# A gated GELU feed-forward kernel: the opening loads dealt out as two equal lines, and five w_down blocks in two transfers each

## The chip, the cores and the metric

The kernel runs on one core of a Trainium2 chip. The metric is the device time of one execution in microseconds (us); lower is better. The kernel before takes 591.58 us, the median of three runs that lie between 591.08 and 591.84 us. One further execution was taken with the hardware profiler on; all durations below come from that one.

## The reference

The inputs are bfloat16: x of 2048 tokens by 1024, w_gate and w_up of 1024 by 3584, w_down of 3584 by 1024.

```python
def _gelu(x):
    return jax.nn.gelu(x, approximate=True)

def reference(x, w_gate, w_up, w_down):
    g = jnp.einsum("bsd,df->bsf", x, w_gate)
    u = jnp.einsum("bsd,df->bsf", x, w_up)
    h = _gelu(g) * u
    return jnp.einsum("bsf,fd->bsd", h, w_down)
```

Three matrix products, with a gated GELU between the first two and the third. The GELU is the tanh form, which the kernel computes as the gate value times a sigmoid of a cubic in it.

## The kernel before, in words

The tokens are worked in two halves of 1024, each in two chunks of 512. For a half, the kernel first computes the hidden values h (kept transposed in `hT`, hidden features on the partitions) and then the output rows of that half.

**Hidden values.** The 3584 hidden features are 28 blocks of 128, in eight groups of 3, 3, 3, 3, 4, 4, 4, 4 blocks (`GROUPS`). For one block and one chunk, eight matmuls of 128x512 (one for each 128 of the 1024 model dimensions, index `ko`, function `mm1`, L103) add up the gate value in one PSUM bank, and eight more the up value in another. ScalarE (ACT) and VectorE (DVE) then form GELU(gate) x up in five operations (class `Evac`) and write it to `hT`. The weights of a group stand in one of three ring buffers (`wg`, `wu`) and are loaded ahead by SyncE's DMA queue (SP), one transfer of gate and one of up weights for a group (`wload`, L89).

**Output.** For each 128 tokens and each 512 output columns, 28 matmuls with `hT` as the stationary side and `wd` (w_down, seven blocks of four 128-row slices each) as the moving side fill one bank (`down`, L306); the bank is copied and stored (`store`). The seven `wd` blocks are loaded once, one 1 MB transfer each, between the weight prefetches of the first half (L326).

**The order of the work.** The schedule is by hand: each engine's and each queue's instructions run in the order in which the program names them. DMAs are issued from two queues, SP and ACT's own (ACT's DMA issues stand in ACT's program order between its other instructions). A DMA signals its landing on one of eight DMA semaphores, which are handed out in turn; a DMA that takes over a semaphore waits until that semaphore's last DMA has landed.

**The opening,** which the change is about. The moving side of the first products is x transposed (`xT`). For the first chunk, six of the eight 128-wide slices of x are loaded plainly, in three pieces `xn` of 512 tokens by 256 (`xpart`, L186), and turned on TensorE: the function `turn(ko)` makes four 128x128 transposes against an identity matrix (L230) into a PSUM bank, and DVE copies them into `xT` (L236; for `ko` = 0 in two copies of 256 columns each, L239 and L240). The last two slices come by transposing DMA (`xload`, L98). The weights of group 0 come in single slices of 128x384 for `ko` 0 to 3 and in double slices after that (`wpart`, L192). The fifteen opening loads are dealt to the two queues in a hand-written order (L200 to L214): SP has the first x piece (all 512 tokens), then an up slice, the second x piece, and so on; ACT has the first two gate slices, an up slice, the third x piece, and so on.

Before the data is there, TensorE runs six filler matmuls on constants (`dummy`, L174; `NWARM`). ACT loads its activation table (L180) and does one 1-element Square on the tile `gate` (L181), which DVE has zeroed (L178, 128x512 bfloat16); ACT's later DMA issues stand behind these two in its program. In `first_group`, TensorE runs `turn(0)`, two more fillers of 512 and 256 columns while DVE copies, the three gate matmuls of `ko` = 0, `turn(1)`, the three up matmuls of `ko` = 0, and then for each further `ko` two matmuls, the next `turn`, and four matmuls. The loop that sets this order:

```python
            for i, (b, j) in enumerate(steps):
                mm1(ps[j][b], (wg, wu)[b], j, 0, ko)
                if i == (2 if ko == 0 else 1) and ko + 1 < NTURN:
                    turn(ko + 1)
```

Of the kernel before, what the change touches and what calls it, by code (L numbers as in the profile page):

```python
# [14 lines left out]
def kernel(  # L15
# [36 lines left out]
    NTMP = 3  # L52
    NST = 4
    WDF = 4
    NWARM = 6
    NTURN = 6
    TPC = SCH // P

    pool = ctx.enter_context(tc.tile_pool(name="sb", bufs=1))
# [39 lines left out]
            out=xT[c][ko], in_=x2[s0 : s0 + SCH, ko * P : (ko + 1) * P]  # L99
        )  # L100

    def mm1(ps, w, j, c, ko):
        nc.tensor.matmul(  # L103
            ps,
            lhsT=w[:, ko, j * P : (j + 1) * P],
            rhs=xT[c][ko],
            start=(ko == 0),
            stop=(ko == NKB - 1),
        )

# [56 lines left out]

    ctx.enter_context(tc.manual_schedule())

    gate = pool.tile([P, SCH], bf16, name="gate")  # L170
    gated = pool.tile([P, 1], f32, name="gated")

    def dummy(b, n=SCH):
        nc.tensor.matmul(b[:, :n], lhsT=warm[:, :P], rhs=warm[:, :n], start=True, stop=True)  # L174

    nc.vector.memset(gate, 0.0)  # L178
    make_identity(nc, ident)
    nc.scalar.preload_act_table(ACT.Sigmoid)  # L180
    nc.scalar.activation(gated, gate[:, :1], ACT.Square)  # L181
    for _ in range(NWARM):
        dummy(banks[5])

    def xpart(eng, ko, n):
        eng.dma_start(  # L186
            out=xn[ko // 2][:, :, (ko % 2) * P : (ko % 2 + n) * P],
            in_=x2[0:SCH, ko * P : (ko + n) * P].rearrange("(t p) d -> p t d", p=P),
        )

    def wpart(eng, ring, w, ko, n):
        eng.dma_start(  # L192
            out=ring[0][:, ko : ko + n, : GROUPS[0] * P],
            in_=w[ko * P : (ko + n) * P, : GROUPS[0] * P].rearrange("(ko ki) f -> ki ko f", ki=P),
        )


    S, A = nc.sync, nc.scalar
    G, U = (wg_ring, w_gate), (wu_ring, w_up)
    xpart(S, 0, 2)  # L200
    wpart(A, *G, 0, 1)
    wpart(S, *U, 0, 1)
    wpart(A, *G, 1, 1)
    wpart(A, *U, 1, 1)
    xpart(S, 2, 2)
    xpart(A, 4, 2)
    wpart(S, *G, 2, 1)
    wpart(S, *U, 2, 1)
    wpart(S, *G, 3, 1)
    wpart(A, *U, 3, 1)  # L210
    wpart(S, *G, 4, 2)
    wpart(A, *U, 4, 2)
    wpart(S, *G, 6, 2)
    wpart(A, *U, 6, 2)  # L214
    for ko in range(NTURN, NKB):
        xload(0, 0, ko)
    for n in (1, 2):
# [32 lines left out]
    def first_group():  # L250
        wg, wu = wg_ring[0], wu_ring[0]
        ps = [(bank(), bank()) for _ in range(GROUPS[0])]
        turn(0)
        dummy(banks[5])
        dummy(banks[5], SCH // 2)
        n0 = GROUPS[0]
        for ko in range(NKB):
            steps = [(b, j) for j in range(n0) for b in range(2)]
            if ko == 0:
                steps = [(b, j) for b in range(2) for j in range(n0)]  # L260
            for i, (b, j) in enumerate(steps):
                mm1(ps[j][b], (wg, wu)[b], j, 0, ko)
                if i == (2 if ko == 0 else 1) and ko + 1 < NTURN:
                    turn(ko + 1)
        e = [Evac(ps[j][0], ps[j][1], j, 0) for j in range(GROUPS[0])]
        e[0].square()
        e[1].square()
        e[0].cubic()
        e[0].sigmoid()
        e[1].cubic()  # L270
        e[2].square()
        e[0].gelu()
        e[0].product()
        e[1].sigmoid()
        e[2].cubic()
        e[1].gelu()
        e[1].product()
        e[2].sigmoid()
        e[2].gelu()
        e[2].product()  # L280
# [34 lines left out]
    for half in range(NHALF):  # L315
        base = half * NG
        if half == 0:
            first_group()
            group(1, [0], ahead=2)
            group(2, [0])  # L320
            for g in range(NG):
                group(g, [1] if g < NW else range(HSC))
                i = g - 1
                if 0 <= i < len(wd):
                    for q in range(i, len(wd) if g == NG - 1 else i + 1):
                        nc.sync.dma_start(  # L326
                            out=wd[q],
                            in_=w_down[q * WDF * P : (q + 1) * WDF * P, :].rearrange(
                                "(fo fi) d -> fi fo d", fi=P
                            ),  # L330
                        )
                prefetch(g + 3)
        else:
            for g in range(NG):
                group(base + g, range(HSC))
                prefetch(base + g + 3)
        k = 0
        xnext = [(c, ko) for c in range(HSC) for ko in range(NKB)] if half + 1 < NHALF else []
        for ss in range(HS // P):
            for dc in range(NDC):  # L340
                last = half == NHALF - 1 and ss == HS // P - 1 and dc == NDC - 1
                if last:
                    down(half, ss, dc * DMW, DMW // 2, 1)
                    down(half, ss, dc * DMW + DMW // 2, P, 1)
                    down(half, ss, dc * DMW + DMW - P, P, 0)
                else:
                    down(half, ss, dc * DMW, DMW, k)
                k += 1
                if xnext:
                    c, ko = xnext.pop(0)  # L350
                    xload(half + 1, c, ko)
# [30 lines left out]
```

## Time and profile before

| what | value |
|---|---|
| median of three runs | 591.58 us (591.08 to 591.84) |
| the profiled execution's own time | 591.7 us |
| its span, first to last instruction | 589.9 us |
| TensorE (PE) busy | 583.4 us, 99% |
| DVE busy / ACT busy | 244.2 us (41%) / 147.7 us (25%) |
| matmuls of the gate and up products (L103), mean | 380 and 379 ns |
| matmuls of the output (L306), mean | 366 ns |
| fillers (L174), mean | 601 ns |
| first matmul with real data / last instruction on PE | 4.86 us / about 587.3 us |

How to read it: a duration of one matmul overlaps that of the next, so the pace of a row of matmuls is the distance between their starts (for 128x512, about 0.216 us in nearly all of the span), not the mean duration. "PEld" is TensorE's loading of the stationary side, which runs beside the matmuls. "SPq" and "ACTq" are the DMA issues of the two queues; their durations are those of the issue, not of the transfer.

### The profile page before, as it was taken

How to read it: one execution, taken by the hardware profiler on the slowest of the kernel's cores; microseconds unless marked ns; L12 is line 12 of the kernel's file. 1: busy time of each engine (PE TensorE's matmuls, PEld its weight loads, DVE VectorE, ACT ScalarE, POOL GpSimd, SP SyncE). 2: the span in 40 equal slices, each digit the busy share in tenths (PEclk: the TensorE clock that was granted, in tenths of full speed). 3: DMA queues.
4: the chain of work that ended last, by engine and by line, in shares of the span. 5: the costliest groups of instructions: out<-in, count | busy, mean ns of one | idle time of the engine just before them, and what ended most of it. 6: DMA issues, size and time to landing. Idle time of an engine off the chain costs nothing.

```text
span 589.9 us, 6587 instructions
## 1 busy us (share of the span) xinstructions
PE 583.4 (99%) x2723; PEld 269.0 (46%) x2776; DVE 244.2 (41%) x361; ACT 147.7 (25%) x243; POOL 0.7 (0%) x6
## 2 busy tenths in 40 slices
PE   9999999999999999999999999999999999999998
PEld 4444444444444444444444444444444444444445
DVE  1765665565656400000046565656556562000000
ACT  1433333333333200000023333333333331000000
POOL 0000000000000000000000000000000000000000
PEclk9999999999999999999999999999999999999999
DMA  8906936055050311111203034214000000000000
GB/s 233 222 10 186 316 104 214 13 202 178 1 178 1 107 48 42 45 46 36 54 19 108 17 126 143 86 57 131 12 1 1 1 2 9 19 27 19 27 19 27
DMA packets 57789, 45.51 MB, mean 77 GB/s; under 512 B 15776, under 2 KB 54176, under 8 KB 57760
## 3 DMA queue, kind: packets, MB, share of 16 engines
q1 hardware_dynamic: 56112, 44.05, 24.8%
q10 hardware_dynamic: 1648, 1.05, 0.6%
q8 instruction: 21, 0.34, 0.2%
q14 instruction: 8, 0.07, 0.0%
HBM read 37.49 MB, written 4.19 MB: 71 GB/s over the span
## 4 chain that ended last, share of the span: by engine, by line
PE 98%; DMA 1%; issue 0%; ACT 0%
PE bank L103 65%; PE bank L306 33%; DMA xn<-in_x_dram 1%; PE bank L230 0%; PE bank L174 0%; ACT st L298 0%
## 5 line engine op out<-in xcount | busy, mean ns | idle before, releaser
L103 PE MATMUL bank<-xT,wg 128*128 128x512 bf16 x880 | 213.8, 380 | 0.9
L103 PE MATMUL bank<-xT,wu 128*128 128x512 bf16 x876 | 212.6, 379 | 1.0
L306 PE MATMUL bank<-wd,hT 128*128 128x512 bf16 (+2 forms) x935 | 193.0, 366 | 0.9
L306 PEld LDWEIGHTS <-hT 128*128 128x128 bf16 x952 | 90.9, 98 | 102.9
L103 PEld LDWEIGHTS <-wg 128*128 128x128 bf16 x896 | 87.8, 98 | 105.6 <-issue 0.6
L103 PEld LDWEIGHTS <-wu 128*128 128x128 bf16 x896 | 87.7, 98 | 105.0
L125 ACT ACTIVATE sq<-bank 128x512 f32<-128x512 f32 x112 | 66.7, 596 | 172.7 <-PE bank L103 166.8
L136 DVE TENSOR_TENSOR tt<-sg,bank 128x512 bf16<-128x512 bf16 x112 | 77.0, 687 | 75.9 <-ACT sg L133 75.8
L128 DVE SCALAR_TENSOR_TENSOR wq<-sq,bank 128x512 f32<-128x512 f32 x112 | 76.9, 687 | 65.2 <-ACT sq L125 65.2
L133 ACT ACTIVATE sg<-wq 128x512 bf16<-128x512 f32 x112 | 70.5, 629 | 88.3 <-DVE wq L128 88.3
L300 DVE CAST st<-bank 128x512 bf16<-128x512 f32 (+2 forms) x17 | 11.1, 652 | 178.3 <-PE bank L306 166.9
L139 DVE TENSOR_TENSOR hT<-tt,bank 128x512 bf16<-128x512 bf16 x112 | 77.0, 687 | 12.4 <-DVE tt L136 0.9
L298 ACT CAST st<-bank 128x512 bf16<-128x512 f32 (+1 forms) x17 | 9.6, 566 | 178.1 <-PE bank L306 178.1
L236 DVE COPY xT<-bank 128x512 bf16<-128x512 bf16 x5 | 2.1, 425 | 6.2 <-PE bank L230 6.2
L174 PE MATMUL bank<-const-bfloat16-1.0 128*128 128x512 bf16 (+1 forms) x8 | 3.6, 601 | 0.8 <-PEq L366 0.8
L230 PEld LDWEIGHTS <-xn 128*128 128x128 bf16 x24 | 2.1, 111 | 2.7 <-DMA xn<-in_x_dram 1.2
L230 PE MATMUL bank<-ident,xn 128*128 128x128 bf16 x24 | 2.7, 247 | 0.3 <-DMA xn<-in_x_dram 0.3
L174 PEld LDWEIGHTS <-const-bfloat16-1.0 128*128 128x128 bf16 x8 | 1.0, 138 | 1.8 <-issue 1.8
L239 DVE COPY xT<-bank 128x256 bf16<-128x256 bf16 x1 | 0.3, 292 | 3.1 <-PE bank L230 3.1
L180 ACT ACT_TABLE_LOAD x1 | 1.3, 1283 | 0.7 <-PEq L366 0.7
L178 DVE MEMSET gate<- 128x256 uint32 x1 | 0.3, 272 | 0.9 <-PEq L366 0.9
masks.py:199 POOL TENSOR_SCALAR_AFFINE_SELECT ident<-ident 128x128 bf16<-128x128 bf16 x1 | 0.3, 292 | 0.1
(7 smaller groups left out, 1.1 us busy)
## 6 DMA issues: line engine op xcount, KB each, us to landing
wg<-in_w_gate_dram SPq DMA_DIRECT2D x8, 1024.0 KB, 5.4
wu<-in_w_up_dram SPq DMA_DIRECT2D x8, 1024.0 KB, 7.0
wd<-in_w_down_dram SPq DMA_DIRECT2D x7, 1024.0 KB, 8.8
wg<-in_w_gate_dram SPq DMA_DIRECT2D x7, 768.0 KB, 4.7
wu<-in_w_up_dram SPq DMA_DIRECT2D x7, 768.0 KB, 6.6
out_dram<-st SPq DMA_DIRECT2D x31, 128.0 KB, 1.7
xn<-in_x_dram SPq DMA_DIRECT2D x2, 256.0 KB, 4.0
xT<-in_x_dram SPq DMA_TRANSPOSE x26, 2.6
```

The costliest lines, as they stand in the source:

```text
L103: nc.tensor.matmul(ps, lhsT=w[:, ko, j * P : (j + 1) * P], rhs=xT[c][ko], start=(ko == 0), stop=(ko == NKB - 1),)
L125: nc.scalar.activation(self.sq, self.g, ACT.Square, scale=GELU_SQRT_C)
L128: nc.vector.scalar_tensor_tensor(out=self.wq, in0=self.sq, scalar=1.0, in1=self.g, op0=ALU.add, op1=ALU.mult)
L133: nc.scalar.activation(self.sg, self.wq, ACT.Sigmoid, scale=GELU_K)
L136: nc.vector.tensor_tensor(out=self.tt, in0=self.sg, in1=self.g, op=ALU.mult)
L139: nc.vector.tensor_tensor(out=self.dst, in0=self.tt, in1=self.u, op=ALU.mult)
L174: nc.tensor.matmul(b[:, :n], lhsT=warm[:, :P], rhs=warm[:, :n], start=True, stop=True)
L230: nc.tensor.transpose(tp[t // (TPC // 2)][:, t * P : (t + 1) * P], xn[ko // 2][:, t, (ko % 2) * P : (ko % 2 + 1) * P], ident,)
L236: nc.vector.tensor_copy(out=xT[0][ko], in_=tp[0][:, :SCH])
L298: nc.scalar.copy(out=st[:, :cw], in_=ps[:, :cw])
L300: nc.vector.tensor_copy(out=st[:, :cw], in_=ps[:, :cw])
L306: nc.tensor.matmul(ps[:, :cw], lhsT=hT[f][:, ss * P : (ss + 1) * P], rhs=wd[f // WDF][:, f % WDF, c0 : c0 + cw], start=(f == 0), stop=(f = ...
```

## The change

- **Opening loads.** Each of the three x pieces is issued as two transfers: the first 256 tokens by SP, the last 256 tokens by ACT (`xhalves`). All gate slices of group 0 go by SP, all up slices by ACT. Both queues thus have the same list: x half, slice 0, slice 1, x half, slice 2, slice 3, x half, slices 4-5, slices 6-7. There are 18 opening loads in place of 15.
- **ACT's start.** The table load and the 1-element Square come after ACT's first x half and ahead of its other loads. The `gate` tile that the Square waits for is twice as long (128x1024).
- **TensorE's opening.** `NWARM` goes from 6 to 7, but the loop runs `NWARM - 1` times, so there are six fillers as before. The two fillers after `turn(0)` are of 256 and 128 columns in place of 512 and 256. The three gate matmuls of `ko` = 0 become six of 256 columns: first the first 256 tokens for the three blocks, then the last 256 tokens. `turn(1)` still follows the gate matmuls.
- **w_down.** Five of the seven `wd` blocks are loaded as two transfers of two slices each (`NSPLIT = 5`); the other two stay whole.

In the compiled changed kernel, the semaphore waits of the opening loads are these. On SP, the first five loads wait for nothing, the sixth (gate slice 3) waits for one half of the first x piece, the third x half for gate slice 0, gate slices 4-5 for SP's half of the second x piece, gate slices 6-7 for gate slice 2. On ACT, the first three wait for no DMA (the second and third stand behind the Square), the half of the second x piece waits for a half of the first, up slice 2 for gate slice 1, up slice 3 for up slice 0, the half of the third x piece for up slice 1, up slices 4-5 for the half of the second x piece, up slices 6-7 for up slice 2. From the stores of the first half on, each transfer has the same semaphore as before, since the added transfers are eight in all.

```diff
-    NWARM = 6
+    NWARM = 7
     NTURN = 6
+    NSPLIT = 5
...
-    def mm1(ps, w, j, c, ko):
+    def mm1(ps, w, j, c, ko, t0=0, t1=SCH):
         nc.tensor.matmul(
-            ps,
+            ps[:, t0:t1],
             lhsT=w[:, ko, j * P : (j + 1) * P],
-            rhs=xT[c][ko],
-            start=(ko == 0),
+            rhs=xT[c][ko][:, t0:t1],
+            start=(ko == 0 and t0 == 0),
             stop=(ko == NKB - 1),
         )
...
-    gate = pool.tile([P, SCH], bf16, name="gate")
+    gate = pool.tile([P, 2 * SCH], bf16, name="gate")
...
-    nc.scalar.preload_act_table(ACT.Sigmoid)
-    nc.scalar.activation(gated, gate[:, :1], ACT.Square)
-    for _ in range(NWARM):
+    for _ in range(NWARM - 1):
         dummy(banks[5])
-    def xpart(eng, ko, n):
+    def xpart(eng, ko, n, t0=0, t1=TPC):
         eng.dma_start(
-            out=xn[ko // 2][:, :, (ko % 2) * P : (ko % 2 + n) * P],
-            in_=x2[0:SCH, ko * P : (ko + n) * P].rearrange("(t p) d -> p t d", p=P),
+            out=xn[ko // 2][:, t0:t1, (ko % 2) * P : (ko % 2 + n) * P],
+            in_=x2[t0 * P : t1 * P, ko * P : (ko + n) * P].rearrange("(t p) d -> p t d", p=P),
         )
...
+    def xhalves(ko, n):
+        xpart(S, ko, n, 0, TPC // 2)
+        xpart(A, ko, n, TPC // 2, TPC)
+
     G, U = (wg_ring, w_gate), (wu_ring, w_up)
-    xpart(S, 0, 2)
-    wpart(A, *G, 0, 1)
-    wpart(S, *U, 0, 1)
-    wpart(A, *G, 1, 1)
-    wpart(A, *U, 1, 1)
-    xpart(S, 2, 2)
-    xpart(A, 4, 2)
-    wpart(S, *G, 2, 1)
-    wpart(S, *U, 2, 1)
-    wpart(S, *G, 3, 1)
-    wpart(A, *U, 3, 1)
-    wpart(S, *G, 4, 2)
-    wpart(A, *U, 4, 2)
-    wpart(S, *G, 6, 2)
-    wpart(A, *U, 6, 2)
+    xhalves(0, 2)
+    nc.scalar.preload_act_table(ACT.Sigmoid)
+    nc.scalar.activation(gated, gate[:, :1], ACT.Square)
+    for ko in (0, 1):
+        wpart(S, *G, ko, 1)
+        wpart(A, *U, ko, 1)
+    xhalves(2, 2)
+    for ko in (2, 3):
+        wpart(S, *G, ko, 1)
+        wpart(A, *U, ko, 1)
+    xhalves(4, 2)
+    for ko in (4, 6):
+        wpart(S, *G, ko, 2)
+        wpart(A, *U, ko, 2)
...
-        dummy(banks[5])
         dummy(banks[5], SCH // 2)
+        dummy(banks[5], P)
...
-            steps = [(b, j) for j in range(n0) for b in range(2)]
+            steps = [(b, j, 0, SCH) for j in range(n0) for b in range(2)]
             if ko == 0:
-                steps = [(b, j) for b in range(2) for j in range(n0)]
-            for i, (b, j) in enumerate(steps):
-                mm1(ps[j][b], (wg, wu)[b], j, 0, ko)
-                if i == (2 if ko == 0 else 1) and ko + 1 < NTURN:
+                h = SCH // 2
+                steps = [(0, j, t, t + h) for t in (0, h) for j in range(n0)]
+                steps += [(1, j, 0, SCH) for j in range(n0)]
+            for i, (b, j, t0, t1) in enumerate(steps):
+                mm1(ps[j][b], (wg, wu)[b], j, 0, ko, t0, t1)
+                if i == (2 * n0 - 1 if ko == 0 else 1) and ko + 1 < NTURN:
                     turn(ko + 1)
...
-                        nc.sync.dma_start(
-                            out=wd[q],
-                            in_=w_down[q * WDF * P : (q + 1) * WDF * P, :].rearrange(
-                                "(fo fi) d -> fi fo d", fi=P
-                            ),
-                        )
+                        n = WDF // 2 if q < NSPLIT else WDF
+                        for f in range(0, WDF, n):
+                            r = (q * WDF + f) * P
+                            nc.sync.dma_start(
+                                out=wd[q][:, f : f + n, :],
+                                in_=w_down[r : r + n * P, :].rearrange("(fo fi) d -> fi fo d", fi=P),
+                            )
```

## The prediction, made before the changed kernel was run

> **What bounds the kernel now.** I read the page's busy shares first, then the chain of work that ended last.
>
> ```profile
> PE 583.4 (99%) x2723; PEld 269.0 (46%) x2776; DVE 244.2 (41%) x361; ACT 147.7 (25%) x243; POOL 0.7 (0%) x6
> ...
> PE bank L103 65%; PE bank L306 33%; DMA xn<-in_x_dram 1%; PE bank L230 0%; PE bank L174 0%; ACT st L298 0%
> ```
>
> TensorE carries the span. The one other thing on the chain is the load of an x piece. The chain in order of time says where:
>
> ```profile
> 0.67 0.07 issue
> 0.74 3.03 DMA xn<-in_x_dram
> 3.81 0.61 PE bank L230 x4
> 4.42 0.64 PE bank L174 x2
> 5.06 1.28 PE bank L103 x3
> 6.34 0.38 PE bank L230 x4
> ```
>
> After 3.81 us nothing but TensorE stands on it until the last store. So only the opening can be shortened, and a late transfer can only cost there if TensorE comes to stand still. The timeline of the opening (start, duration, engine, line, operation):
>
> ```profile
> 0.74 0.45 SPq L186 DMA_DIRECT2D xn<-in_x_dram  x1
> ...
> 0.77 2.72 PE L174 MATMUL bank<-const-bfloat16-1.0 128*128 128x512 bf16 x6 [0.77 <-PEq L366]
> ...
> 3.79 0.39 ACTq L186 DMA_DIRECT2D xn<-in_x_dram  x1
> ...
> 3.81 0.61 PE L230 MATMUL bank<-ident,xn 128*128 128x128 bf16 x4 [0.32 <-DMA xn<-in_x_dram]
> ...
> 4.22 0.84 PE L174 MATMUL bank<-const-bfloat16-1.0 128*128 128x512 bf16 x2
> ...
> 4.25 0.29 DVE L239 COPY xT<-bank 128x256 bf16<-128x256 bf16 x1 [3.12 <-PE bank L230]
> ...
> 4.86 1.48 PE L103 MATMUL bank<-xT,wg 128*128 128x512 bf16 x3
> ...
> 6.14 0.58 PE L230 MATMUL bank<-ident,xn 128*128 128x128 bf16 x4
> ...
> 6.56 0.81 PE L103 MATMUL bank<-xT,wu 128*128 128x512 bf16 x3
> ...
> 7.67 0.39 PE L230 MATMUL bank<-ident,xn 128*128 128x128 bf16 x4
> ```
>
> To be seen: x lands at 3.77 (0.74 + 3.03), TensorE's turn starts at 3.81. The first copy ends at 4.25 + 0.29 = 4.54, but the first real matmul comes only at 4.86, as the two fillers end there (4.22 + 0.43 + 0.21). Up to 6.14 matmuls run at half pace: three take (6.14 - 4.86) / 3 = 0.427 us each, against (6.99 - 6.56) / 2 = 0.215 later. The switch falls near 6.5. So a start moved forward by d within this slow stretch puts d of work at half pace ahead of the switch and saves only d / 2.
>
> The queues' view of the first 40 us, one value per us, and the time from issue to landing of the three x loads:
>
> ```profile
> GB/s 0 17 190 340 229 335 327 291 285 331 249 55 192 328 346 353 332 328 325 327 334 308 83 65 261 113 99 131 119 59 85 0 0 0 0 0 0 0 0 0
> ...
> DMA to landing us min/median/max: 3.0/4.2/5.0
> ```
>
> From 3 to 11 us the engines move about 300 GB/s; before 3 us they are not full.
>
> **The change part by part.** All against the profiled execution: 591.7 us, its span of 589.9 and 1.8 around it; it stands 0.12 over the median.
>
> *Fillers and the first matmuls.* The fillers shrink from 0.64 to 0.32 us, so they end at 4.22 + 0.32 = 4.54, and the first half matmul needs only the first copy, also done at 4.54. The hand-over from DVE to TensorE is hidden here; I take 0.06 us, from the distance of the end of the last 0.11 us transpose of the first half to the copy's start, bounds 0 and 0.2. The start comes at 4.60, 0.26 earlier: worth 0.13 at half pace (0.03 to 0.16). Six matmuls of 256 columns take 6 x 0.213, as three of 512 take 3 x 0.427: nothing. They load weights three more times; a weight load is 0.15 us here and the transposes, at 0.107 us each with a load of their own, hide theirs, so nothing (upper bound 3 x 0.15 uncovered, half of it 0.22).
>
> *The first x piece on two queues.* Both halves are issued at 0.74 (ACT's program now begins with its half). By 3 us 17 + 190 = 207 KB had moved, of the 262 KB of the piece, and the third microsecond ran at 190 against 340 in the fourth. If the second line fills that room, the piece comes up to 0.4 us sooner; TensorE could use 0.5, as its six fillers end at 0.77 + 0.38 + 5 x 0.427 = 3.29. If the start was slow for a reason that two lines share, it lands at 3.77 as now. Against it, SP's gate slice 0 (98 KB, 0.3 us at 330 GB/s) is now right behind SP's half and competes with ACT's half: up to 0.3 later. So -0.4 to +0.3 on landing; I take 0.2 earlier, between a full gain and none, since the slow stretch is visible: worth 0.10 (0.20 to -0.15).
>
> The rule that speaks against it: the Trainium skill, page "DMA: Bandwidth & Descriptors", section "Rules for kernel authors", says of two transfers to disjoint halves not to bother, since both run over the same sixteen engines and only interleave, and that spreading over issuing engines saves issue time alone. By that rule the 0.10 is gone and the sum is 591.45; the row with 190 GB/s leaves both open.
>
> *The weights of ko = 0 and 1.* Gate slice 0 landed by 4.1 before the first matmul at 4.86. Now SP sends it behind 131 KB rather than beside 262 KB; the bytes ahead of its end are no more than before, so about 4.1, against 4.40 needed. Up slice 0 is needed only at about 6.1.
>
> *ACT's start.* Its table load (1.28 us) moves behind an issue of 0.45; ACT has no other work until the first Square at 16.31. The doubled memset (0.27 to 0.54 us, starting at 0.86) ends at 1.40 instead of 1.13 and with the Square behind it holds ACT's next issue, as 1.17 follows 1.13 now. Up slice 0 thus goes out at 1.44. Nothing: 4.6 us lie between that and its use.
>
> *The second x piece.* SP's half goes out at about 2.3, like the whole piece now (1.79). ACT's half waits for a first half to land, at about 3.6, as ACT's x load now waits until 3.79. From issue to landing the x loads take 3.0 to 5.0; the issues of 98 KB on ACT 2.9 to 4.4. With 131 KB on a short queue I take 3.1, near the low end (the first gate slice 2.9, the first x piece 3.0): landed at 6.7. TensorE wants it at 7.67 less about 0.25, 7.4. Margin 0.7; at 5.0 it is late by 1.2 and that counts in full, since by then the pace is full. Behind it on ACT queue up slices 2 and 3, the third x half and the double slices; if all are 1 us later, up slices 4-5 (9.05 landed before, used at 12.01) still have cover. Nothing, bounds 0 and +1.2.
>
> *SP and its followers.* SP has nine opening issues ahead of the transposing loads instead of eight (0.45 us more), but its waits are for loads that land no later than those it waits for now. The transposing loads start at 7.70, take 1.25 us each to issue and 2.8 to land, so the second is there at about 11.7; their slices are first used at 14.60 and 15.90. The gate weights of group 1 were issued at 10.23 and landed 5.7 us later, near 15.9; their first use is at 17.19. Half a microsecond later still fits. Nothing.
>
> *w_down in two.* Five more issues of 0.57 us on SP between 48 and 130 us, where SP stands mostly in waits for TensorE (238 us in its waits). Queued behind one is the weight prefetch of a group two ahead: it needs 5 to 7 us to land, and a group takes at least 3 x 16 x 0.216 = 10.4. The blocks are first read at 200 us. Nothing; the bound is one missed prefetch, for which no wait on L103 speaks (1.0 us idle in all).
>
> Sum: -0.13 - 0.10 = -0.23. From 591.70 that is 591.47; less the 0.12 by which that execution stood over the median, **591.35**.
>
> **The rivals.**
>
> *A, the forecast:* a quarter of a microsecond from an earlier start. For it: fillers end 0.32 after the first copy. 591.0 to 591.5.
>
> *B, two lines bring nothing:* the first piece lands at 3.77 or later, the start gains only the fillers. 591.45, with the upper landing bound 591.6. For it: ACT's first weight slice, issued at 1.17, took 2.9 us to land, beside SP's 3.0, though smaller; against it, the 190 GB/s.
>
> *C, slower, the second x piece:* ACT's half is now issued some 1.8 us after the whole piece was. If it takes 5.0 us, it lands at 8.6, TensorE stands for 1.2 us at `turn(2)`: 592.55. It decides when the landing passes 7.4 + 0.23, that is when the half takes more than 4.0 us. For it: the piece issued at 1.79 did take 5.0. Against it: that one was twice as long and stood behind other loads, and here ACT has only two slices of 98 KB ahead. The boundary of slower by 0.2% lies at 5.2 us.
>
> *D, the switch to full pace falls elsewhere:* it came at 6.5 here, 5.7 us after the first filler and 2.7 after TensorE's pause that ended at 3.81. If the pause resets it, a shorter pause brings it sooner; if it has nothing to do with the kernel's start, it moves from run to run. Full pace from the first matmul on would save (6.5 - 4.4) / 2 = 1.05 more: 590.3; 1.5 us later would cost 0.75: 592.1. The spread of the three runs, 0.76 us, fits such movement.
>
> The Trainium skill, page "TensorE: Matmul & The Clock Gate", section "What's actually happening", has the pace released by a free-running window of 3.4 us; by it the instant is chance and not moved by this change. The 2.7 and 5.7 us above neither confirm nor exclude that.
>
> **How the numbers follow.** A change of 0.2%, 1.18 us, is about what a measurement of this kernel can tell from none; all of A and B and most of the others lie inside it. A 0.50, B 0.22, C 0.15 (0.06 of it beyond +1.18), D 0.13 (0.06 of it beyond -1.18 and 0.01 beyond +1.18). So faster 0.06, same 0.87, slower 0.07. The predicted time is A's, 591.35. The range 590.6 to 592.1 holds A and B, C with a stall up to 0.75 us and the middle of D, and leaves out the rest of C (0.09) and of D (0.08).
>
> **What would show it.** The first transposes at about 3.6, the first real matmul near 4.4 with 256 columns, at half pace; a pause of TensorE before 3.6 of about 0.3 us; no DMA wait on TensorE after that; `turn(2)` near 7.4; the rest of the span like before, shifted by 0.2 to 0.3. Transposes at 3.8 mean B. A wait of TensorE on an x piece near 7.4 means C. Half pace ending well off 6.5 means D. A wait on L103 or L306 after 17 us would make the whole working wrong.

## The result, and the profile after

Against the same kernel before, the changed kernel is slower: 592.41 us in the median of 22 runs, 591.11 for the kernel before in as many; the ratio is 1.0022, 95% interval 1.0016 to 1.0029. That is 1.3 us (0.9 to 1.7). The forecast was 591.35, with a range up to 592.1. The three runs shown ahead of the prediction stood high: over 22 runs the kernel before lies at 591.11, not 591.58.

The first profile of the changed kernel (span 593.3 us, 595.04 us in all, the longest of its runs) shows three waits on loads, where the kernel before had none after 3.81 us. From its page, the busy shares, the chain, and one group of matmuls with the idle time ahead of it:

```profile
PE 584.1 (98%) x2726; PEld 269.1 (45%) x2779; DVE 244.4 (41%) x361; ACT 147.8 (25%) x243; POOL 0.7 (0%) x6
...
PE bank L107 64%; PE bank L315 32%; DMA wu<-in_w_up_dram 1%; DMA xn<-in_x_dram 1%; PE bank L236 0%; ACT st L307 0%
...
L107 PE MATMUL bank<-xT,wu 128*128 128x512 bf16 x877 | 213.9, 380 | 2.3 <-DMA wu<-in_w_up_dram 1.3
```

The chain in order of time (start, duration, what) no longer leaves the loads at 3.81 us, but at 13.7:

```profile
0.74 2.43 DMA xn<-in_x_dram
3.19 3.85 DMA xn<-in_x_dram
7.06 6.62 DMA wu<-in_w_up_dram
13.73 0.61 PE bank L107
```

The first is SP's half of the first x piece, which lands at 3.17 and for which ACT's next x load waits; the second is ACT's half of the second x piece, the third the load of up slices 4-5. The timeline shows the queues and TensorE's waits:

```profile
3.19 0.42 ACTq L186 DMA_DIRECT2D xn<-in_x_dram  x1
...
3.29 0.44 PE L236 MATMUL bank<-ident,xn 128*128 128x128 bf16 x4
...
4.00 0.81 PE L107 MATMUL bank<-xT,wg 128*128 128x256 bf16 x6
...
6.87 2.50 SPq L101 DMA_TRANSPOSE xT<-in_x_dram  x2
7.06 1.13 ACTq L192 DMA_DIRECT2D wu<-in_w_up_dram  x2
...
7.08 0.28 PE L236 MATMUL bank<-ident,xn 128*128 128x128 bf16 x2 [0.83 <-DMA xn<-in_x_dram]
...
11.03 0.28 PE L236 MATMUL bank<-ident,xn 128*128 128x128 bf16 x2 [0.74 <-DMA xn<-in_x_dram]
...
13.73 0.61 PE L107 MATMUL bank<-xT,wu 128*128 128x512 bf16 x1 [1.33 <-DMA wu<-in_w_up_dram]
```

TensorE starts on real data earlier than before (4.00 against 4.86), then stands in `turn(2)` and `turn(4)` for ACT's halves of x, and, longest, in the matmuls of `ko` = 4 for up slices 4-5. These were issued at 7.06, just behind SP's transposing loads (6.87), and needed 6.6 us to land. In the kernel before, the last three loads of ACT's line, up slices 3, 4-5 and 6-7, all went out ahead of the transposing loads:

```profile
4.22 2.71 ACTq L192 DMA_DIRECT2D wu<-in_w_up_dram  x3
...
7.70 2.50 SPq L98 DMA_TRANSPOSE xT<-in_x_dram  x2
```

The stretches of this profile and of the kernel before (stretch, its length, busy time of each engine in the order PE, PEld, DVE, ACT, POOL, then granted clock, DMA share, GB/s) show what that did to the loads, and a second thing. The changed kernel:

```profile
4.00:9.00 5.00, 4.17 (x31) 2.47 (x31) 1.06 (x4) 0.00 (x0) 0.00 (x0) 1.00 0.88 248
9.00:14.00 5.00, 2.88 (x15) 1.17 (x15) 0.78 (x2) 0.00 (x0) 0.00 (x0) 0.96 1.17 174
14.00:17.00 3.00, 3.00 (x11) 1.33 (x10) 0.42 (x1) 0.00 (x0) 0.00 (x0) 0.50 1.07 293
```

The same stretches of the kernel before:

```profile
4.00:9.00 5.00, 5.00 (x28) 2.60 (x27) 1.35 (x4) 0.00 (x0) 0.00 (x0) 1.00 1.01 293
9.00:14.00 5.00, 4.95 (x33) 2.64 (x33) 1.27 (x3) 0.00 (x0) 0.00 (x0) 1.00 0.92 231
14.00:17.00 3.00, 3.00 (x16) 1.35 (x15) 0.06 (x1) 0.69 (x2) 0.00 (x0) 1.00 1.08 344
```

The loads bring 248 and 174 GB/s where they brought 293 and 231. And after the waits TensorE ran at half pace, a granted clock of 0.50, from 13.63 to 17.04 us. That second loss belongs to this execution: the next profile does not have it.

### The profile page after: what moved, and what is told of

The parts are those of the page before. It is cut to its first block, busy times and chain, and to the rows that moved or that the text cites. A ratio compares the mean times of both kernels' runs of the same rounds, so it can differ in the third digit from the quotient of the medians.

```text
span 593.3 us, 6601 instructions
## 1 busy us (share of the span) xinstructions
PE 584.1 (98%) x2726; PEld 269.1 (45%) x2779; DVE 244.4 (41%) x361; ACT 147.8 (25%) x243; POOL 0.7 (0%) x6
## 4 chain that ended last, share of the span: by engine, by line
PE 97%; DMA 2%; issue 0%; ACT 0%
PE bank L107 64%; PE bank L315 32%; DMA wu<-in_w_up_dram 1%; DMA xn<-in_x_dram 1%; PE bank L236 0%; ACT st L307 0%
## 5 line engine op out<-in xcount | busy, mean ns | idle before, releaser
L107 PE MATMUL bank<-xT,wg 128*128 128x512 bf16 (+1 forms) x882 | 213.7, 379 | 1.0
L178 PE MATMUL bank<-const-bfloat16-1.0 128*128 128x512 bf16 (+2 forms) x8 | 3.0, 531 | 0.8 <-PEq L376 0.8
```

What stands on the lines that cost most here:

```text
L107: nc.tensor.matmul(ps[:, t0:t1], lhsT=w[:, ko, j * P : (j + 1) * P], rhs=xT[c][ko][:, t0:t1], start=(ko == 0 and t0 == 0), stop=(ko == NKB ...
```

## The experiments

"u4-5" is the load of up slices 4-5, "xT" are SP's two transposing loads of the first chunk. Times are medians of 5 to 11 executions where nothing else is said, ratios are against the kernel before on the same chip, with 95% intervals, and what is read from a trace comes from one execution.

**The changed kernel once more,** unedited.

> The changed kernel once more, unedited, for a second profile. The first one shows TensorE waiting 0.95 us in turn(2), 0.9 us in turn(4) and 1.3 us on an up slice, then half pace from 13.6 to 17.0 us, and its execution took 595.04 us. Theory L (the ACT line's late loads): the same waits on loads that ACT issues appear again, in all 1 to 2 us after 5 us, whatever the pace does, and the execution takes 592 to 593. Theory K (the clock alone): no wait of more than 0.3 us after 5 us, the half pace just ends later than 6.5 us.

Measured: 593.24 us in its one, profiled execution, a little over the 592 to 593 of theory L. Like the first, it is slower than the median of 592.41, so the waits of both may be longer than usual. Its chain, and the end of its longest wait:

```profile
1.76 3.96 DMA wg<-in_w_gate_dram
5.71 0.02 issue
5.73 0.34 ACTq L192
6.07 0.04 issue
6.11 0.44 ACTq L192
6.55 0.04 issue
6.59 0.45 ACTq L186
7.04 0.04 issue
7.08 6.42 DMA wu<-in_w_up_dram
```

```profile
13.55 0.39 PE L107 MATMUL bank<-xT,wu 128*128 128x512 bf16 x1 [1.21 <-DMA wu<-in_w_up_dram]
```

u4-5 is the wait again, 1.6 us from matmul to matmul (11.95 to 13.55), with no half pace behind it; `turn(4)` waits 0.4 us (10.54 to 10.97), and the wait in `turn(2)` is gone here, as TensorE came there only at 7.45. The chain also says why u4-5 went out so late: gate slice 1 lands at 5.72; up slice 2 on ACT has waited for just that; behind it follow up slice 3, the x half and u4-5, one issue after the other, up to 7.08. (In the first profile u4-5 had to wait for the half of the second x piece, landed at 7.04.) Theory L stands.

**TensorE's new opening alone.** On the kernel before:

```diff
...
-        dummy(banks[5])
         dummy(banks[5], SCH // 2)
+        dummy(banks[5], P)
...
-                steps = [(b, j) for b in range(2) for j in range(n0)]
...
+                steps = [(0, j, t, t + h) for t in (0, h) for j in range(n0)]
+                steps += [(1, j, 0, SCH) for j in range(n0)]
...
```

> The kernel before with TensorE's new opening alone (fillers of 256 and 128 columns, six half matmuls); loads, ACT's start and w_down as before. By the prediction's first term it is 0.13 us faster than before (0.03 to 0.16). Theory P (the added matmuls and the shorter fillers cost) has it slower, by up to 0.5. Theory L has nothing on this one.

Measured: 590.95 us, before 591.05; ratio 1.0001 (0.9992 to 1.0010). No gain that can be measured. Its profile shows what took its place:

```profile
4.31 0.81 PE L104 MATMUL bank<-xT,wg 128*128 128x256 bf16 x6
...
6.62 0.39 PE L104 MATMUL bank<-xT,wu 128*128 128x512 bf16 x1 [0.38 <-DMA wu<-in_w_up_dram]
```

TensorE starts at 4.31, gets through ten matmuls, and waits until 6.6 for up slice 1, which the old list lands at 6.57. In the old list that load is the next limit behind the start; the profile of w_down alone, below, has the same wait at 6.85.

**The loads alone.** The changed kernel with TensorE's old opening and whole w_down blocks:

```diff
-    NSPLIT = 5
+    NSPLIT = 0
...
+        dummy(banks[5])
         dummy(banks[5], SCH // 2)
-        dummy(banks[5], P)
...
-                steps = [(0, j, t, t + h) for t in (0, h) for j in range(n0)]
-                steps += [(1, j, 0, SCH) for j in range(n0)]
...
+                steps = [(b, j) for b in range(2) for j in range(n0)]
...
```

> The changed kernel's opening loads and ACT start, with TensorE's old opening and whole w_down blocks. Theory L: the loss is here, slower by 1.0 to 1.4 us, with TensorE waiting on loads that ACT issues. Theory W (w_down in two costs, or the semaphores that it shifts): within 0.3 us of before. Theory P: within 0.3 us of before or faster.

Measured: 592.80 us; ratio 1.0024 (1.0015 to 1.0033). The whole loss is here, 1.7 us, more than the 1.0 to 1.4 expected. u4-5, issued at 6.91, landed at 12.86; TensorE stood 1.2 us from matmul to matmul for it, and 0.7 us in `turn(4)`.

**w_down alone.** The kernel before with `NSPLIT = 5`:

```diff
...
+                        n = WDF // 2 if q < NSPLIT else WDF
+                        for f in range(0, WDF, n):
...
```

> The kernel before with five w_down blocks in two transfers each, nothing else. Theory L and the prediction: within 0.2 us of before. Theory W: slower by 0.5 to 1.3 us, with a wait on L103 or L306 after 40 us.

Measured: 591.31 us; ratio 1.0004 (0.9996 to 1.0013), and no wait on a matmul after 7 us. Theory W falls.

**No transposing load in the opening.** Slices 6 and 7 of x come as a fourth pair of plain halves:

```diff
-    NTURN = 6
+    NTURN = 8
...
-    xn = [pool.tile([P, TPC, 2 * P], bf16, name=f"xn{q}") for q in range(NTURN // 2)]
+    xn = [pool.tile([P, TPC, 2 * P], bf16, name=f"xn{q}") for q in range(3)]
...
+    xn.append(gate.rearrange("p (t d) -> p t d", t=TPC))
...
-    for ko in (4, 6):
-        wpart(S, *G, ko, 2)
-        wpart(A, *U, ko, 2)
+    wpart(S, *G, 4, 2)
+    wpart(A, *U, 4, 2)
+    xhalves(6, 2)
+    wpart(S, *G, 6, 2)
+    wpart(A, *U, 6, 2)
```

> The changed kernel, but slices 6 and 7 of x come as a fourth pair of plain halves and are turned on TensorE, so that no transposing load runs in the first 13 us. It pays 8 more transposes, 2 x 0.22 us. The largest wait of the changed kernel is on up slices 4-5: issued on ACT at 7.06, landed at 13.5 to 13.7. Theory X (SP's two transposing loads, issued from 6.9 on, slow ACT's last loads): up slices 4-5 land within 4 us of their issue, near 11, TensorE's wait on them is gone, and the time is 591.4 to 591.9 with the 0.44 paid. Theory I (their issue is late, as it waits for the half of the second x piece to land at 7.0): they still land after 12, and the time is 592.6 to 593.

Measured: 594.54 us; ratio 1.0057 (1.0043 to 1.0071). Both forecasts of the time missed. u4-5 landed 4.7 us after its issue (7.22 to 11.95), later than the 4 us of theory X, and TensorE did not wait for it, as theory X had it; but the waits moved to ACT's other loads:

```profile
7.25 0.28 PE L239 MATMUL bank<-ident,xn 128*128 128x128 bf16 x2 [0.67 <-DMA xn<-in_x_dram]
9.50 0.39 PE L107 MATMUL bank<-xT,wu 128*128 128x512 bf16 x1 [0.89 <-DMA wu<-in_w_up_dram]
14.83 0.28 PE L239 MATMUL bank<-ident,gate 128*128 128x128 bf16 x2 [0.27 <-DMA gate<-in_x_dram]
16.71 0.39 PE L107 MATMUL bank<-xT,wu 128*128 128x512 bf16 x1 [0.52 <-DMA wu<-in_w_up_dram]
```

The last of ACT's line, up slices 6-7, took 6.4 us (10.25 to 16.67). With no transposing loads to issue, SP went on at 7.88 with the weights of group 1, 768 KB each. So without transposing loads there is still a late load at the end of ACT's line, now beside the weights of group 1. That these weights delay it is likely, but not shown; and the wait at 9.50, for an up slice issued at 5.63, began before most of group 1 was issued.

**The second x piece ahead of `ko` = 1:**

```diff
-    for ko in (0, 1):
-        wpart(S, *G, ko, 1)
-        wpart(A, *U, ko, 1)
+    def w(ko, n):
+        wpart(S, *G, ko, n)
+        wpart(A, *U, ko, n)
+
+    w(0, 1)
     xhalves(2, 2)
...
+    w(1, 1)
...
```

> The changed kernel with the second x piece's halves ahead of the slices of ko = 1, so that ACT's half goes out at about 1.9 us without a wait, and up slice 1 waits in its place for the first x half. Theory I: up slices 4-5 then wait for up slice 1, which lands at about 6, and come 1 us earlier; the time is 591.3 to 591.8. Theory X: they are issued 1 us earlier but still run beside the transposing loads and land after 12; the time stays within 0.3 us of 592.4. In both, no wait on x in turn(2), but one on up slice 1 near 5.8.

Measured: 592.88 us; ratio 1.0027 (1.0018 to 1.0035). The wait in `turn(2)` is gone, and none on up slice 1 shows, but ACT's line is no earlier: up slice 1 waits for a half of the first x piece until 3.70, up slice 2 for SP's half of the second until 6.07, and u4-5 goes out at 7.45, beside xT (7.43), not 1 us earlier as both theories had it. It lands at 12.9, and TensorE stands 0.8 us from matmul to matmul for it. The time is over both forecasts, nearer to theory X. The half of the second x piece is not what decides.

**u4-5 on SP,** ahead of xT:

```diff
-    for ko in (4, 6):
-        wpart(S, *G, ko, 2)
-        wpart(A, *U, ko, 2)
+    wpart(S, *G, 4, 2)
+    wpart(S, *U, 4, 2)
+    wpart(S, *G, 6, 2)
+    wpart(A, *U, 6, 2)
```

> The changed kernel with up slices 4-5 on SP behind gate slices 4-5, so ahead of the transposing loads in the same queue. Both theories: they land near 10.5, TensorE's wait of 1.3 to 1.8 us on them is gone, and the time is 591.0 to 591.5. If the time stays near 592.4, the wait is not what costs, and both theories fall.

Measured: 592.00 us; ratio 1.0012 (1.0003 to 1.0020): part of the loss is gone, less than expected. u4-5 lands at 11.55, not near 10.5, and the wait on it is gone, but the half of the third x piece, last but one on ACT, is now the late one: issued at 6.08, landed at 11.22, 0.9 us of standing in `turn(4)`.

**A swap in the old list,** on the kernel with TensorE's opening alone:

```diff
-    wpart(A, *U, 1, 1)
-    xpart(S, 2, 2)
+    wpart(S, *U, 1, 1)
+    xpart(A, 2, 2)
     xpart(A, 4, 2)
```

> The kernel before with TensorE's new opening (as in the run with that alone, 590.95 us) and one swap in its list of loads: up slice 1 goes by SP in the second x piece's place, the second x piece by ACT in up slice 1's. In the run with the opening alone, TensorE waited 0.5 us for up slice 1, landed at 6.57. If that landing is what holds the old list's opening: up slice 1 lands by 5.5, the next wait is for the second x piece, at 6.8 to 7.0, and the time is 0.2 to 0.4 us under 590.95. If not: 590.9 to 591.2.

Measured: 592.02 us; ratio 1.0015 (1.0006 to 1.0024), against the forecast of a gain. Up slice 1 landed at 5.99, not by 5.5, the second x piece at 7.49, not by 7.0. The profiled execution has the switch to full pace at 6.7, as late as the profile before, and the same span (589.9 us); its 592.75 us hold 2.8 us outside the span, the kernel before 1.8. The spans of all eleven executions have a median of 590.2 us, against 589.3 of the kernel before beside them, so the others do lose inside the span. TensorE waits little in the profiled one (0.15 us on a matmul for the first x piece, 0.5 us of weight loading for group 1), so where they lose is not shown. What it shows is ACT's line going late here too: up slice 3, which now waits for gate slice 2 (landed at 6.77), goes out at 6.79 instead of 4.22, and u4-5 at 7.18, just ahead of xT (7.31). It lands at 11.16, and nothing waits for it.

**ACT's loads ahead of its table load:**

```diff
     xhalves(0, 2)
-    nc.scalar.preload_act_table(ACT.Sigmoid)
-    nc.scalar.activation(gated, gate[:, :1], ACT.Square)
     for ko in (0, 1):
...
     for ko in (4, 6):
         wpart(S, *G, ko, 2)
         wpart(A, *U, ko, 2)
+    nc.scalar.preload_act_table(ACT.Sigmoid)
+    nc.scalar.activation(gated, gate[:, :1], ACT.Square)
```

> The changed kernel, but ACT's table load and Square come after all of ACT's opening loads. ACT then issues four loads without a wait instead of three (SP four instead of five): its half of the second x piece goes out near 2.2 us instead of 3.2 to 3.5. Theory I (ACT's line is late by its issues, from that first wait on): the half lands near 6, up slices 4-5, whose issue waits for a landing of that stage, go out near 6 instead of 7 and land before 11; no wait in turn(2), the wait on up slices 4-5 under 0.5 us, time 591.0 to 591.5. If the issue does not matter, 592.2 to 592.6.

Measured: 591.37 us; ratio 1.0003 (0.9995 to 1.0012), an interval below that of the changed kernel. Of 1.3 us, 1.0 comes back. ACT's and SP's issues in this run:

```profile
2.27 0.46 ACTq L186 DMA_DIRECT2D xn<-in_x_dram  x1
...
6.88 0.91 ACTq L192 DMA_DIRECT2D wu<-in_w_up_dram  x2
```

```profile
7.78 2.50 SPq L101 DMA_TRANSPOSE xT<-in_x_dram  x2
```

The x half goes out at 2.27 instead of 3.19 to 3.48. But u4-5 goes out at 6.88, hardly earlier than in the changed kernel (7.06); what differs is that xT goes out 0.9 us *after* it and not before, since SP now has four loads without a wait and not five. u4-5 lands in 4.2 us, at 11.12, and TensorE waits for nothing after 7 us. The expectation had the time right and the reason in part: the x half landed at 6.86, not near 6, and it was not u4-5's issue. But xT is not all that differs: ACT's loads ahead of u4-5 also landed sooner, up slice 3 at 7.76 (9.61 and 9.35 in the changed kernel's two profiles) and the half of the third x piece at 8.98 (10.98 and 10.92). This run does not tell the two apart; the holds below do: in the three that leave ACT's issues alone these two land at 9.1 to 9.6 and at 10.4 to 10.7, hardly sooner than in the changed kernel.

**SP held until ACT's line has landed,** by an 8-byte load into up slices 6-7 ahead of xT:

```diff
+    r = (NKB - 1) * P
+    S.dma_start(out=wu_ring[0][0:1, NKB - 1, GROUPS[0] * P - 4 : GROUPS[0] * P], in_=w_up[r : r + 1, GROUPS[0] * P - 4 : GROUPS[0] * P])
     for ko in range(NTURN, NKB):
         xload(0, 0, ko)
```

> The changed kernel with one added transfer of 8 bytes on SP ahead of the transposing loads, into a corner of up slices 6-7, so that SP has to wait until these have landed before it sends anything further. Theory F (what SP sends after its own line, first the transposing loads and then the weights of group 1, takes the engines from ACT's lagging line): up slices 4-5, issued at 7.0 as before, land within 4 us, by 11, the wait of 1.3 to 1.8 us on them shrinks under 0.4, and the time is 591.2 to 591.7, unless the transposing loads now come too late for 14.6 us. Theory I alone: they still land after 12 and the time is 592.4 or more.

Measured: 594.66 us; ratio 1.0069 (1.0055 to 1.0084). The wait on u4-5 is gone (issued 7.20, landed 12.03, 4.8 us, so a little later than expected), but SP was held until 12.85, too late for the first transposing load (landed at 15.53, with 0.6 us of standing from matmul to matmul), and TensorE stood 2.45 us from matmul to matmul for the weights of group 1. In its profile half pace followed that wait, from 21.27 to 24.68.

**Whole x pieces:**

```diff
     def xhalves(ko, n):
-        xpart(S, ko, n, 0, TPC // 2)
-        xpart(A, ko, n, TPC // 2, TPC)
+        xpart(A if ko == 2 else S, ko, n)
```

> The changed kernel with whole x pieces (first and third by SP, second by ACT), 15 opening loads; all gate slices by SP and all up slices by ACT as changed. It tells the halving from the dealing out by kind. If the halving costs (three more loads on the same eight semaphores, so each waits for an earlier landing one step sooner): 591.0 to 591.5. If the dealing by kind costs (ACT ends behind SP whatever the x pieces do): 592.2 to 593.

Measured: 592.18 us; ratio 1.0018 (1.0009 to 1.0026). Between the two forecasts, at the lower edge of the second. The profile (of an execution of 591.67 us, under the median) has one wait, 1.3 us from matmul to matmul in `turn(2)` for the second x piece, which ACT issued at 2.34 behind two up slices and which took 5.1 us. So the loss is not bound to the halving: with whole pieces ACT's line is late at another place.

**SP held until the third x piece has landed,** ACT's issues untouched; an 8-byte copy that nobody waits for:

```diff
+    S.dma_start(out=gate[0:1, SCH : SCH + 4], in_=xn[2][0:1, TPC - 1, 0:4])
     for ko in range(NTURN, NKB):
         xload(0, 0, ko)
```

> The changed kernel with one added 8-byte copy on SP ahead of the transposing loads, from the third x piece's ACT half into an unused part of gate, so that SP waits until that half has landed (10.1 to 11.0 in the changed kernel) and nobody waits for the copy. ACT's issues stay as changed. Theory F (SP's transposing loads take the engines from ACT's last loads): the wait of 1.3 to 1.8 us on up slices 4-5 goes, the waits of 0.3 to 1.0 us in turn(2) and turn(4) stay, and the time is 591.5 to 592.0; the transposing loads land by 14.6. Theory I alone: up slices 4-5 land after 12.5 still, and the time is 592.4 or more.

Measured: 593.78 us; ratio 1.0050 (1.0038 to 1.0063). On u4-5 theory F is right: issued at 6.79, landed at 11.16 (4.4 us), no wait. (The copy takes a semaphore too, so that u4-5 waits for gate slice 3 and not for the x half; its issue moves by 0.3 us at most in this run and the next holds, its landing by over 2 us.) On the time it missed, as the price is taken elsewhere: 0.55 us in `turn(2)` and 0.67 us for an up slice at 9.0, both on ACT's loads, and the most at the start of group 1. SP's issue, and TensorE at the start of group 1:

```profile
11.56 2.51 SPq L101 DMA_TRANSPOSE xT<-in_x_dram  x2
14.11 0.58 SPq L92 DMA_DIRECT2D wg<-in_w_gate_dram  x1
```

```profile
17.05 0.38 PE L107 MATMUL bank<-xT,wu 128*128 128x512 bf16 x1
19.05 0.82 PE L107 MATMUL bank<-xT,wg 128*128 128x512 bf16 x3 [1.62 <-DMA wg<-in_w_gate_dram]
```

**Both edits together** (ACT's loads first, SP held behind the third x piece):

> The changed kernel with ACT's table load and Square behind ACT's loads (591.37 alone) and SP held until the third x piece's ACT half has landed. If the early transposing loads still cost something there, 590.7 to 591.1, so as fast as the kernel before or faster; if ACT's earlier loads had settled it all, 591.2 to 591.6; if the hold makes the weights of group 1 late, over 592 with a wait on them near 17 us.

Measured: 592.20 us; ratio 1.0026 (1.0014 to 1.0039). The third case of the expectation: no wait on the opening loads (u4-5 lands at 10.40), and 2.0 us from matmul to matmul on the weights of group 1.

**Shorter holds,** ACT's issues untouched: the same copy, from up slice 2 (`wu_ring[0][0:1, 2, 0:4]`) and from up slice 3.

> As the run with SP held behind the third x piece, but the copy reads a corner of up slice 2, which lands at 7.7 to 8.0, so the transposing loads go out near 8.7 instead of 6.9 to 7.0. Theory F: up slices 4-5, still issued near 7, land before 12, the wait on them is under 0.5 us, the group 1 weights come in time, and the time is 591.3 to 591.9. Theory I: the wait stays over 1 us and the time is 592.2 or more.

> The same with a corner of up slice 3, which lands at 9.3 to 9.6; the transposing loads go out near 10.3, between the run above and the one with the third x piece (11.6). Theory F: no wait on up slices 4-5; the group 1 weights go out near 12.9 and are late by 0.5 to 1 us; the time is 592.0 to 592.8.

Measured: 592.34 us, ratio 1.0016 (1.0007 to 1.0025), and 593.06 us, ratio 1.0029 (1.0018 to 1.0041). In both, u4-5 lands at 11.2 and nothing waits for it. ACT's and SP's issues in the first, and TensorE's first two matmuls of `ko` = 4:

```profile
6.99 0.93 ACTq L192 DMA_DIRECT2D wu<-in_w_up_dram  x2
...
9.59 2.51 SPq L101 DMA_TRANSPOSE xT<-in_x_dram  x2
...
11.62 0.38 PE L107 MATMUL bank<-xT,wg 128*128 128x512 bf16 x1
11.84 0.38 PE L107 MATMUL bank<-xT,wu 128*128 128x512 bf16 x1
```

On the wait theory F is right in both, on the time it missed in both (591.3 to 591.9, and 592.0 to 592.8). Up slice 2 landed at 8.72 in the first, later than expected, so xT went out at 9.59 and TensorE stood 0.5 us from matmul to matmul for group 1's gate weights; in the second 1.3 us. The first one's interval overlaps that of the changed kernel: its time shows no sure gain.

Put side by side (issue and landing in us, from the traces):

| kernel | xT out | u4-5 out | u4-5 landed | took | ratio |
|---|---|---|---|---|---|
| before | 7.70 | 5.01 | 9.05 | 4.0 | 1 |
| TensorE's opening alone | 7.72 | 4.83 | 9.33 | 4.5 | 1.0001 |
| w_down alone | 7.66 | 5.42 | 9.28 | 3.9 | 1.0004 |
| swap in the old list | 7.31 | 7.18 | 11.16 | 4.0 | 1.0015 |
| changed, first profile | 6.87 | 7.06 | 13.68 | 6.6 | 1.0022 |
| changed, second profile | 7.04 | 7.08 | 13.50 | 6.4 | |
| loads alone | 6.88 | 6.91 | 12.86 | 5.9 | 1.0024 |
| x2 ahead of ko = 1 | 7.43 | 7.45 | 12.93 | 5.5 | 1.0027 |
| u4-5 on SP | 7.49 | 6.09 | 11.55 | 5.5 | 1.0012 |
| ACT's loads first | 7.78 | 6.88 | 11.12 | 4.2 | 1.0003 |
| whole x pieces | 7.42 | 6.42 | 10.58 | 4.2 | 1.0018 |
| SP behind up slice 2 | 9.59 | 6.99 | 11.24 | 4.3 | 1.0016 |
| SP behind up slice 3 | 9.99 | 7.33 | 11.17 | 3.8 | 1.0029 |
| SP behind third x piece | 11.56 | 6.79 | 11.16 | 4.4 | 1.0050 |
| both edits | 9.91 | 6.73 | 10.40 | 3.7 | 1.0026 |
| SP behind ACT's line | 12.85 | 7.20 | 12.03 | 4.8 | 1.0069 |
| no transposing load | none | 7.22 | 11.95 | 4.7 | 1.0057 |

Where xT goes out before u4-5, if only by 0.02 us, u4-5 takes 5.5 to 6.6 us and TensorE waits; where u4-5 goes out first on ACT (by 0.13 us in the swap, by 0.9 us and more in the others), it takes 3.7 to 4.8 us, and nothing waits for it. One row does not fit: u4-5 on SP went out 1.4 us ahead of xT and took 5.5 us, though no wait came of it. The holds, which move xT and leave ACT's issue of u4-5 within 0.3 us of where it was, show that the early followers of SP make the largest wait. How the 1.3 us split between that wait and ACT's other late loads is not shown: every hold that removed the wait moved SP's later loads too, and paid there. The one edit that took both the wait and most of the loss away, ACT's loads first, changed more than xT.

## Why the prediction was wrong, point by point

- **The step that failed** is "SP and its followers", set at nothing, together with the clause that up slices 4-5 "still have cover". I asked whether SP's followers would come too late, and only that, and reckoned them half a microsecond later. They went out earlier, at 6.87 and 7.04 instead of 7.70, since SP's next loads wait for its half of the second x piece, landed at 5.46 and 6.09, where the whole piece landed at 6.74. u4-5, at 5.01 before, went out at 7.06 and 7.08. In the old list nothing of ACT's line was still to be issued when xT went out; now two double slices were. u4-5 landed 4.4 to 4.6 us later than before, against a cover of 3.0 (9.05 landed, 12.01 used), and TensorE stood 1.6 to 1.7 us from matmul to matmul, 0.2 us of which a matmul takes anyway. No term of the sum had a price for that.
- **The second x piece** was taken to land at 6.7 and landed at 7.04 and 6.88. Near enough, but TensorE came for it at 6.1 in the execution with the early switch of pace, not at 7.4, and stood for 1.05 us from matmul to matmul; in the other it did not wait. So the wait that rival C names came in one profile of two, and the largest wait in both is on another load of the same queue: its price, 592.55, is close to the measured time by luck.
- **The first x piece on two queues.** I took 0.2 us. In twelve profiles with halves, the later half landed between 3.34 and 3.99, at 3.71 in the mean; in five with a whole piece by SP it landed between 3.56 and 3.77, at 3.63 in the mean. So halves bring nothing, and the first profile's 3.34 was the best of its kind. Rival B's premise was right. The rule of the Trainium skill, page "DMA: Bandwidth & Descriptors", section "Rules for kernel authors", that spreading over issuing engines does not help bandwidth, agrees with that; its row on two transfers is about halves of the partitions, and the halves here are tokens, on all partitions.
- **Fillers and half matmuls.** The hand-over from DVE came out as taken: the first copy ended at 3.65 + 0.29 = 3.94, the first half matmul started at 4.00. Alone they measured nothing (a ratio of 1.0001, medians 0.1 us apart) for 0.13 forecast; what I had not seen is that up slice 1 lands at 6.5 to 6.8 in the old list, so that an earlier start runs into it. At slow pace it was hidden (used at 7.45), and the profile I worked from had the slow pace up to 6.5.
- **The switch to full pace (rival D).** It moves from run to run: 3.4 us (changed), 3.7 (TensorE's opening alone, w_down alone), 4.2, 4.4, 4.6, 4.9, 5.4, 6.3, 6.5 (before), 6.6 and 6.7 in the other profiles that record the clock, with the same six fillers from 0.77 on; in the five that do not, the distances of the matmuls put it between 3.4 and 6.8 too. And where a profile records more than one switch, these lie 3.41 us or a whole multiple of it apart: 3.39, 13.63 and 17.04 in the first, 4.20, 21.27 and 24.68 in the run with SP held until ACT's line had landed. The free-running window of 3.4 us that the Trainium skill has, page "TensorE: Matmul & The Clock Gate", section "What's actually happening", fits both. So the instant is chance, as far as these profiles tell. But the price was too high: w_down alone had the switch at 3.7 and took 591.31 us, the kernel before at 6.5 and took 591.70, so 2.8 us sooner goes with at most 0.4, as the loads take over.
- **ACT's start.** The table load and the memset delayed what I said, up slice 0 to 1.44, and that had its cover. Not seen: of the eight semaphores that are free at the start, SP's loads take five and ACT's three. I had both lists of waits and counted five and three, and drew nothing from it. The trace of the kernel before has the same five and three; what is new is that ACT has nine loads and not seven, so that six of them, and not four, stand behind a wait. With the table load moved, the split is four and four, and 1.0 us comes back.
- **w_down in two:** nothing, as forecast (1.0004).

## What to carry to other kernels

When two queues share the same engines, cost a new order of loads by what each queue sends *after* its list too: the queue that is done first goes on with later work and takes the engines from the other's last loads. Ask of every step that gets earlier whom it now overtakes, not only of those that get later. And where the loads set the pace, as in this opening, a saving on the compute engine, or holding one queue back, moved the wait to the next load.

## What was not expected of the hardware

- With transposing loads among the plain ones, the engines moved less. Below are the bytes moved in each us (the first value is 0 to 1 us), from the queues' view of two runs. The first is the second profile of the changed kernel, where xT, issued from 7.04 on, landed at 13.2 and 14.6, together with ACT's double slices. The second is the run with SP behind the third x piece, where the plain loads had the engines to themselves until 11.6:

```profile
GB/s 0 5 272 274 212 302 195 203 325 273 130 202 210 118 268 324 328 325 328 324 327 335 319 292 23 196 200 127 105 57 104 131 0 0 0 0 0 0 0 0
```

```profile
GB/s 0 18 270 288 245 271 224 174 314 356 192 8 8 123 131 51 299 375 344 326 326 326 326 335 330 235 21 254 139 129 131 100 43 120 0 0 0 0 0 0
```

  With xT among them, the engines moved 130 to 210 GB/s from 10 to 13 us; plain loads alone 314 and 356 from 8 to 10. The transposing loads alone (13 to 15 us of the second) come to 123 and 131.
- TensorE can fall back to half pace after quite short standing: after waits of 0.95 and 1.7 us within 10.1 to 13.7 the pace was half until 17.04. In the run with SP behind the third x piece a single wait of 2.0 us had no such effect, and in the run with both edits one as long had none. The raster of 3.41 us on which the switches lie says more than the waits do: in the stretch of that length that ends at the fall, TensorE was busy for 1.39 us (10.22 to 13.63) and, in the run with SP held until ACT's line had landed, for 1.34 us (17.86 to 21.27). In the run with both edits the wait of 2.0 us left 1.80 us in its stretch (14.81 to 18.22), and the pace held. These are three cases; that the busy share of a stretch decides, and where the limit lies, is not shown.
